# Attention ahead of two MLP stages: global values copied at a step's end, low words shifted on ScalarE, three working buffers for doubles

## The chip, the cores and the metric

One core of a Trainium2 chip runs the whole program. The metric is the device time of one execution in microseconds (us), the median of several runs. The core's engines work side by side, each through a queue of its own in order: PE (TensorE), DVE (VectorE), ACT (ScalarE), POOL (GpSimd) and SP (SyncE, which only issues DMAs here). An instruction that waits holds up all that stand behind it in its engine's queue.

## The reference

```
scores = q @ k.T / 8, for 4 batches x 8 heads x 768 tokens x 64
keep   = (key < 8, the globals) or (0 <= query - key < 96, the local ones)
a      = softmax(where(keep, scores - slope[head] * distance, -1e9))
x      = (a @ v) as 3072 rows of 512
x      = each row through one of 8 experts (512 -> 1024 -> 512, ReLU),
         chosen by sorting all gate values, 384 rows each
out    = two_sided_leaky(x @ w_in) @ w_out     # 512 -> 2048 -> 512
```

The two matrices of the last stage, w_in and w_out, come in as doubles (64 bits); everything else is float32.

## The kernel before

The program first does the attention (about 220 us), then routes the rows, then sends each expert's rows through both MLP stages. Only the attention part is touched.

Attention runs in 48 steps, two for each tile of 128 tokens (`g`), each with four of the eight heads (`u` is 0 or 1). `attention` writes out by hand the order in which each engine gets its work. In step n the queues hold: the scores of step n+1 (L212, tile a_s) on PE; bias and minimum on DVE (L218, a_sx); four exponentials on ACT (L221, a_p); transposes of the probabilities of step n on PE (L232, a_pt), copied out by DVE (L236) and ACT (L234); the product with the gate of step n-2 (L277, a_cb); the transposes of later keys and queries (L169, a_tp); and the values matmul of step n-1 (L248, a_xp). PE is thus a step or two ahead of what the other engines finish.

A key tile sees 104 older keys, of which the first 8 are replaced by the global ones. `place_globals` (L190, tile a_kz) copies the global keys into their places on POOL, two steps ahead of the scores that read them. `place_values` (L196, tile a_v, 32x256) does the same for the global values: it overwrites the first rows of the tile before the step's own, after the values matmul at the end of the step before has read them; the values matmul at the end of the next step reads what was copied. `divisor` (L259) is a small add on POOL.

The doubles are turned into float32 on the side by `Doubles`, as a generator that `attention` advances twice in a step, in four steps of five (PACE). A job is 128x512 doubles, 32 jobs in all, alternately of w_in and w_out. `load` (L67) brings the raw words to a tile f_raw with three slots. At a step's first advance `begin` takes the magnitude of the high word on ACT (L73, into tile f_t), clamps it on POOL (L74) and shifts the low word on POOL (L75, into tile f_r); L73 stands ahead of the exponentials of step n+1. `finish` of the job before, if that was one of w_in, splits it on POOL into two parts (L87, L88). At the second advance, at the step's end, `join` shifts and merges the high word on DVE (L79, L80) and adds the low one on POOL (L82). f_t and f_r have two buffers each, so L73 of a job waits until the job two before has been read for the last time, by L88 or L82.

SP's queue holds in this order what a step issues: the loads of k and q or of v, the store of finished rows, and L67 for a later job.

Of the kernel before, what the change touches and what calls it, by code (L numbers as in the profile page):

```python
# [12 lines left out]
I32 = mybir.dt.int32  # L13
U32 = mybir.dt.uint32
U16 = mybir.dt.uint16
AF = mybir.ActivationFunctionType
OP = mybir.AluOpType
# [13 lines left out]
class Doubles:  # L31
# [36 lines left out]

    def begin(self, job):
        nc, raw = self.nc, job["raw"]  # L70
        t = job["t"] = self.pool.tile([128, self.WIDTH], I32, name="f64_t")
        r = job["r"] = self.pool.tile([128, self.WIDTH], I32, name="f64_r")
        nc.scalar.activation(t.bitcast(FT), raw[:, :, 1].bitcast(FT), AF.Abs, scale=LIFT)  # L73
        nc.gpsimd.tensor_scalar(t.bitcast(FT), t.bitcast(FT), BIG, FLOOR, op0=OP.min, op1=OP.max)  # L74
        nc.gpsimd.tensor_scalar(r, raw[:, :, 0].bitcast(U32), 2.0 ** -29, 1.0, op0=OP.mult, op1=OP.mult)  # L75

    def join(self, job):
        nc, t = self.nc, job["t"]
        nc.vector.tensor_scalar(t, t, 3, 0x7FFFFFF8, op0=OP.logical_shift_left, op1=OP.bitwise_and)  # L79
        nc.vector.scalar_tensor_tensor(t, job["raw"][:, :, 1], -0x80000000, t, op0=OP.bitwise_and, op1=OP.bitwise_or)  # L80
        dst = t if job["dst"] is None else job["dst"].bitcast(I32)
        nc.gpsimd.tensor_tensor(dst, t, job["r"], op=OP.add)  # L82

    def finish(self, job):
        if job["hi"] is not None:
# [5 lines left out]
def attention(ctx, tc, q, k, v, w_gate, n_global, n_local, ident, x_dram, logits, side, router):  # L91
    nc = tc.nc
# [12 lines left out]
    scale = 1.0 / math.sqrt(D)  # L105
# [17 lines left out]
    def load_kq(g):  # L123
        load(g, (("k", k), ("q", q)), 3)

    def load_v(g):
        b, t = divmod(g, NT)
        load(g, (("v", v),), 4)
        if not t:
            nc.sync.dma_start(vg[C - GW:C - W, b % 2], dram_ap(v, b * H * S * D, [[D, G], [S * D, H], [1, D]]))  # L130
# [16 lines left out]
    for r, c0, base, fill in ((rel, G, W, MASKED), (rel0, 0, 0, float(W)), (rel0, G, -G, MASKED)):  # L147
        n = {0: G}.get(c0, r.shape[1] - c0) if r is rel0 else KW - c0
# [23 lines left out]
    def transpose_k(g):  # L172
        t = g % NT
        nc.scalar.activation(kz[:, :, t * C:(t + 1) * C], transpose_in(T["k", g]), AF.Copy)
# [5 lines left out]
    def place_globals(g, u):  # L180
        b, t = divmod(g, NT)
        if t == 0:
            return
        if t == 1 and u == 0:
            kg = work.tile([C, NP, G], FT, name="a_kg", bufs=2)
            nc.gpsimd.tensor_copy(kg, kz[:, :, :G])
            T["KG", b] = kg
        c0 = t * C - GW
        ps = slice(2 * u, 2 * u + 2)
        nc.gpsimd.tensor_copy(kz[:, ps, c0:c0 + G], T["KG", b][:, ps])  # L190

    def place_values(g, u):
        b, t = divmod(g, NT)
        if t:
            hs = slice(4 * u, 4 * u + 4)
            nc.gpsimd.tensor_copy(T["v", g - 1][:C - W, hs], vg[:, b % 2, hs])  # L196

    def scores(g, u):
        b, t = divmod(g, NT)
        if t:  # L200
            c0, n, bs = t * C - GW, KW, bias
        else:
            c0, n, bs = 0, C, bias0
        ps = [psum.tile([C, 2, KW], FT, name=f"a_s{s}") for s in range(2)]
        if u == 0:
            T["sum", g] = work.tile([C, H], FT, name="a_sum", bufs=3)
            T["mn", g] = work.tile([C, H], FT, name="a_mn", bufs=3)
        for a in range(2):
            p = 2 * u + a
            for s in range(2):  # L210
                r = slice(s * D, (s + 1) * D)
                nc.tensor.matmul(ps[s][:, a, :n], T["Q", g][r, p], kz[r, p, c0:c0 + n], start=True, stop=True)  # L212
        for a in range(2):
            sx = work.tile([C, 2, KW], FT, name="a_sx", bufs=2)
            pr = T["P", g, 2 * u + a] = pbuf[:, 2 * u + a]
            for s in range(2):
                h = 2 * (2 * u + a) + s
                nc.vector.tensor_tensor_reduce(out=sx[:, s, :n], in0=ps[s][:, a, :n], in1=bs[:, h], scale=-scale,  # L218
                                               scalar=BIG, op0=OP.add, op1=OP.min,
                                               accum_out=T["mn", g][:, h:h + 1])  # L220
                nc.scalar.activation(pr[:, s, 2 * C - n:], sx[:, s, :n], AF.Exp, bias=T["mn", g][:, h:h + 1],  # L221
                                     scale=-1.0, accum_out=T["sum", g][:, h:h + 1])
# [34 lines left out]
    def divisor(g, u):  # L257
        e = T["se", g, u] = work.tile([C, 4], FT, name="a_se", bufs=4)
        nc.gpsimd.tensor_scalar(e, T["sum", g][:, 4 * u:4 * u + 4], 1e-9, None, op0=OP.add)  # L259

    def norm(g, u):
        r = T["r", g, u] = work.tile([C, 4], FT, name="a_r", bufs=2)
        nc.vector.reciprocal(r, T.pop(("se", g, u)))

    def store(g):
        nc.sync.dma_start(x_dram[g * C:(g + 1) * C, :], T["xo", g])

    def combine(g, u):
        xt = T.pop(("xt", g, u))
        last = g == NG - 1  # L270
        if last and u:
            ps = psum.tile([C, NP, C], FT, name="a_tp", bufs=2).rearrange("c p d -> c (p d)")
            ps = ps[:, :2 * CB].rearrange("c (a d) -> c a d", a=2)
        else:
            ps = psum.tile([C, 2, CB], FT, name="a_cb")
        for a in range(2):
            nc.tensor.matmul(ps[:, a], xt[:, a], cmb[:, 2 * u + a], start=True, stop=True)  # L277
        if not u:
            T["xo", g] = work.tile([C, HD], FT, name="a_xo", bufs=2)
            T["lp", g] = work.tile([C, H, E], FT, name="a_lp", bufs=2)  # L280
        if not last:
            norm(g, u)
        r = T.pop(("r", g, u))
        rr = r.rearrange("c (a s) -> c a s", a=2)
        xo = T["xo", g].rearrange("c (a s d) -> c a s d", s=2, d=D)[:, 2 * u:2 * u + 2]
        nc.vector.tensor_tensor(
            T["lp", g].rearrange("c (a s) e -> c a s e", s=2)[:, 2 * u:2 * u + 2],
            ps[:, :, C:].rearrange("c a (s e) -> c a s e", s=2),
            rr[:, :, :, None].to_broadcast([C, 2, 2, E]), op=OP.mult)
        if last:  # L290
            for i in range(4):
                nc.scalar.activation(xo[:, i // 2, i % 2], ps[:, i // 2, i % 2 * D:(i % 2 + 1) * D], AF.Copy,
                                     scale=r[:, i:i + 1])
        else:
            nc.vector.tensor_tensor(xo, ps[:, :, :C].rearrange("c a (s d) -> c a s d", s=2),
                                    rr[:, :, :, None].to_broadcast([C, 2, 2, D]), op=OP.mult)
        if u:
            nc.vector.tensor_reduce(logits[:, g, :], T["lp", g].rearrange("c h e -> c e h"), axis=AX.X, op=OP.add)
            if g < NG - 2:
                T["store"] = g  # L300
            else:
                store(g)

    def turn(n):
        return 2 <= n < N - 3 and n % PACE[1] < PACE[0]
# [3 lines left out]
    N = len(steps)  # L309
# [10 lines left out]
    for n in range(N + 2):  # L320
        if n < N:
            g, u = steps[n]
            if u == 0 and n and g + 3 < NG:
                load_kq(g + 3)
            if u == 1 and g + 2 < NG:
                load_v(g + 2)
            if "store" in T:
                store(T.pop("store"))
            nx = steps[n + 1] if n + 1 < N else None
            if n + 2 < N:  # L330
                place_globals(*steps[n + 2])
            place_values(g, u)
            if turn(n):
                next(side)
            if nx:
                scores(*nx)
            transpose_p(g, u, 0)
            transpose_p(g, u, 1)
            divisor(g, u)
            if n >= 2:  # L340
                combine(*steps[n - 2])
            if n and g + 2 < NG:
                (transpose_q if u else transpose_k)(g + 2)
        if n == 0:
            transpose_k(2)
            load_kq(3)
        if n == N:
            norm(*steps[n - 2])
            norm(*steps[n - 1])
        if 1 <= n <= N:  # L350
            values(*steps[n - 1])
        if n == N:
            router.start()
        if n >= N:
            combine(*steps[n - 2])
        if turn(n):
            next(side)
        else:
            next(setup, None)
# [821 lines left out]
```

## Time and profile before

| | us |
|---|---|
| median of 3 runs | 1121.75 (1120.18 to 1121.84) |
| the profiled execution's own time | 1119.95 |
| its span, from the first instruction to the last | 1118.2 |
| granted clock of TensorE, mean over the span | 0.976 |
| busy in the span: PE, DVE, ACT, POOL | 1065.7, 762.9, 385.6, 540.5 |

The profile is of one execution. Busy times are those of an engine's own instructions; an engine that is busy for a small share of the whole can still set the pace of a part. A wait is given with the instruction that ended it.

### The profile page before, as it was taken

Reading aid. Unit: us, or ns where it says so; the run is one execution under the profiler, and the core shown is the slowest. Engines: PE = TensorE matmul, PEld = TensorE weight load, DVE = VectorE, ACT = ScalarE, POOL = GpSimd, SP = SyncE. Lnnn points to the kernel's source line nnn. Section 1 sums busy time; section 2 is a strip of 40 time slices with the busy share of each in tenths; the row PEclk is TensorE's granted clock in tenths of the full one; section 3 lists DMA queues with packets and bytes.
Section 4 is the critical chain, followed back from the end, with each engine's and each line's share of the span. In section 5 each row is a group of like instructions: output and inputs, shape, how many; then the busy total and the mean of one; then the engine's idle time right before and its main releaser. Section 6 shows DMA issues by size and latency. Waiting matters only on the chain.

```text
span 1118.2 us, 19406 instructions
## 1 busy us (share of the span) xinstructions
PE 1065.7 (95%) x6659; PEld 944.2 (84%) x6659; DVE 762.9 (68%) x2228; ACT 385.6 (34%) x969; POOL 540.5 (48%) x652
## 2 busy tenths in 40 slices
PE   8989898869999999999999999999999999999997
PEld 6777677648888998899889988898899999999995
DVE  7989888778897878897789698778753323231321
ACT  7777777503322320232133113211331233123211
POOL 4888878315455823462346325432543354236222
PEclk9999999968999999999999999999999999999999
DMA  9788877114135525441534533533353435434131
GB/s 219 212 218 223 209 202 187 49 46 134 57 132 179 173 83 181 130 160 58 198 96 149 163 123 109 157 135 129 95 180 123 133 108 185 131 116 167 57 131 67
DMA packets 151219, 156.55 MB, mean 140 GB/s; under 512 B 83536, under 2 KB 116304, under 8 KB 151120
## 3 DMA queue, kind: packets, MB, share of 16 engines
q1 hardware_dynamic: 147280, 142.72, 42.3%
q0 software_dynamic: 3840, 12.59, 3.4%
q8 instruction: 53, 0.87, 0.3%
q14 instruction: 46, 0.38, 0.1%
HBM read 134.31 MB, written 20.97 MB: 139 GB/s over the span
## 4 chain that ended last, share of the span: by engine, by line
PE 75%; DVE 12%; POOL 6%; issue 3%; ACT 2%; DMA 2%; SPq 0%; DVEq 0%; POOLq 0%; ACTq 0%
PE m_h L963 23%; PE m_acc L988 23%; PE m_h L923 9%; PE m_acc L950 9%; PE a_s L212 2%; PE a_pt L232 2%; PE a_xp L248 2%; DVE r_thr L564 2%; DVE r_red L778 1%; DVE r_cmp L770 1%; PE r_ps L704 1%; POOL wo L82 1%; ACT a_p L221 1%; PE a_cb L277 1%; PE a_tp L169 1%
## 5 line engine op out<-in xcount | busy, mean ns | idle before, releaser
L973 POOL TENSOR_TENSOR m_g<-m_t,m_g 128x384 fp32r<-128x384 f32 (+1 forms) x144 | 140.2, 973 | 372.1 <-ACT m_g L972 369.1
L988 PE MATMUL m_acc<-m_so,m_g 128*128 128x512 f32 x1152 | 298.7, 399 | 0.4 <-POOL m_spacer L996 0.3
L963 PE MATMUL m_h<-m_y,wi 128*128 128x384 f32 x1536 | 294.4, 341 | 0.0
L963 PEld LDWEIGHTS m_h<-m_y,wi 128*128 128x128 f32 x1536 | 273.3, 189 | 7.5
L988 PEld LDWEIGHTS m_acc<-m_so,m_g 128*128 128x128 f32 x1152 | 209.6, 189 | 35.3 <-POOL m_g L973 0.9
L972 ACT ACTIVATE m_g<-m_t 128x384 fp32r<-128x384 f32 (+1 forms) x144 | 70.5, 490 | 435.6 <-DVE m_t L971 255.1
L891 POOL TENSOR_TENSOR m_s<-m_r,m_s 128x512 fp32r<-128x512 f32 x128 | 166.9, 1308 | 103.5 <-ACT m_s L890 103.2
L970 DVE TENSOR_SCALAR m_t<-m_h,m_al 128x384 f32<-128x384 f32 (+1 forms) x144 | 82.2, 571 | 149.2 <-PE m_h L963 136.1
L950 PE MATMUL m_acc<-m_hh,m_s 128*128 128x384 f32 x768 | 150.3, 340 | 1.3 <-DVE m_hh L927 1.3
L923 PE MATMUL m_h<-m_xt,m_s 128*128 128x384 f32 x768 | 146.1, 338 | 0.0
L923 PEld LDWEIGHTS m_h<-m_xt,m_s 128*128 128x128 f32 x768 | 136.4, 190 | 1.9 <-ACT m_xt L872 0.3
L950 PEld LDWEIGHTS m_acc<-m_hh,m_s 128*128 128x128 f32 x768 | 132.4, 188 | 2.9 <-DVE m_hh L927 1.6
L890 ACT ACTIVATE m_s<-m_r 128x512 fp32r<-128x512 f32 x128 | 79.7, 626 | 98.8 <-PE m_acc L950 34.1
L221 ACT ACTIVATE a_p<-a_sx,a_mn 128x232 f32<-128x232 f32 (+1 forms) x192 | 88.5, 462 | 25.8 <-DVE a_mn L218 25.4
L927 DVE SCALAR_TENSOR_TENSOR m_hh<-m_h,m_hh 128x384 fp32r<-128x384 f32 x64 | 35.4, 552 | 76.8 <-ACT m_hh L926 76.2
L971 DVE SCALAR_TENSOR_TENSOR m_t<-m_h,m_t 128x384 f32<-128x384 f32 (+1 forms) x144 | 73.9, 513 | 4.9
L778 DVE TENSOR_REDUCE r_red<-r_cmp 128x24 bf16<-128x576 bf16 (+1 forms) x97 | 73.9, 761 | 3.4
L218 DVE CUSTOM_DVE_ANT_0 a_sx<-a_s,a_bias 128x232 f32<-128x232 f32 (+1 forms) x192 | 61.4, 374 | 11.6 <-PE a_s L212 9.4
L212 PE MATMUL a_s<-a_kz,a_qz 64*128 64x232 f32 (+1 forms) x384 | 50.2, 381 | 18.7 <-POOL a_kz L190 16.2
L926 ACT ACTIVATE m_hh<-m_h 128x384 fp32r<-128x384 f32 x64 | 31.5, 492 | 95.6 <-PE m_h L923 82.3
L770 DVE TENSOR_TENSOR r_cmp<-r_mk,r_thr 128x576 bf16<-128x576 uint16 x78 | 61.4, 787 | 0.0
L212 PEld LDWEIGHTS a_s<-a_kz,a_qz 64*128 64x128 f32 x384 | 33.2, 193 | 28.6 <-POOL a_kz L190 22.6
(183 smaller groups left out, 1283.3 us busy)
## 6 DMA issues: line engine op xcount, KB each, us to landing
m_so<-wo_pairs SPq DMA_DIRECT2D x112, 512.0 KB, 3.3
m_r<-in_moe_w_dram SPq DMA_DIRECT2D x128, 256.0 KB, 3.0
f_raw<-in_moe_w_in_dram SPq DMA_DIRECT2D x16, 512.0 KB, 4.6
f_raw<-in_moe_w_out_dram SPq DMA_DIRECT2D x16, 512.0 KB, 3.7
wo_pairs<-m_so SPq DMA_DIRECT2D x16, 512.0 KB, 2.6
a_k<-in_k_dram SPq DMA_DIRECT2D x24, 256.0 KB, 4.8
a_q<-in_q_dram SPq DMA_DIRECT2D x24, 256.0 KB, 5.2
a_v<-in_v_dram SPq DMA_DIRECT2D x24, 256.0 KB, 4.8
```

Source lines behind the costliest of these rows:

```text
L212: nc.tensor.matmul(ps[s][:, a, :n], T["Q", g][r, p], kz[r, p, c0:c0 + n], start=True, stop=True)
L221: nc.scalar.activation(pr[:, s, 2 * C - n:], sx[:, s, :n], AF.Exp, bias=T["mn", g][:, h:h + 1], scale=-1.0, accum_out=T["sum", g][:, h:h + 1])
L778: nc.vector.tensor_reduce(red, cmp, axis=AX.X, op=OP.add)
L890: self.nc.scalar.activation(s[:, 0], r, AF.Copy)
L891: self.nc.gpsimd.tensor_tensor(s[:, 1], r, s[:, 0], op=OP.subtract)
L923: nc.tensor.matmul(ps[:, :n], s1[:, a, d], x[:, b, d], start=(d == 0 and i == 0), stop=(d == self.ND - 1 and i == 2))
L950: nc.tensor.matmul(ps[:, :n], s2[:, b, d * 128:(d + 1) * 128], h[:, a], start=(f == 0 and a + b == 0), stop=(last and a == 1))
L963: nc.tensor.matmul(ps[:, :n], self.wi[:, a, d, f * 128:(f + 1) * 128], y[:, b, d], start=(d == 0 and i == 0), stop=(d == self.ND - 1 and i ...
L970: nc.vector.tensor_scalar(t[:, cs], ps[:, cs], 0.0, self.al[:, f:f + 1], op0=OP.min, op1=OP.mult)
L971: nc.vector.scalar_tensor_tensor(t[:, cs], ps[:, cs], 0.0, t[:, cs], op0=OP.max, op1=OP.add)
L973: nc.gpsimd.tensor_tensor(g[:, 1, cs], t[:, cs], g[:, 0, cs], op=OP.subtract)
L988: nc.tensor.matmul(ps, g[:, a, t * 128:(t + 1) * 128], s[:, b], start=(f == 0 and a + b == 0), stop=(last and a == 1))
```

## The change

Three edits. The shift of the low word goes from POOL (L75, tile f_r) to ACT, where it writes its result over the raw words; the add of `join` reads it there, and tile f_r is gone. f_t has three buffers instead of two. The copy of the global values is queued at the end of a step, behind the values matmul of the step before, instead of near its beginning. One line less stands in the file above `attention`, so L73 to L331 of before are one lower in the changed kernel, but for the shift itself, which is L74 there.

```
     def begin(self, job):
         nc, raw = self.nc, job["raw"]
-        t = job["t"] = self.pool.tile([128, self.WIDTH], I32, name="f64_t")
-        r = job["r"] = self.pool.tile([128, self.WIDTH], I32, name="f64_r")
+        t = job["t"] = self.pool.tile([128, self.WIDTH], I32, name="f64_t", bufs=3)
         nc.scalar.activation(t.bitcast(FT), raw[:, :, 1].bitcast(FT), AF.Abs, scale=LIFT)
         nc.gpsimd.tensor_scalar(t.bitcast(FT), t.bitcast(FT), BIG, FLOOR, op0=OP.min, op1=OP.max)
-        nc.gpsimd.tensor_scalar(r, raw[:, :, 0].bitcast(U32), 2.0 ** -29, 1.0, op0=OP.mult, op1=OP.mult)
+        nc.scalar.activation(raw[:, :, 0], raw[:, :, 0].bitcast(U32), AF.Copy, scale=2.0 ** -29)
 
     def join(self, job):
...
-        nc.gpsimd.tensor_tensor(dst, t, job["r"], op=OP.add)
+        nc.gpsimd.tensor_tensor(dst, t, job["raw"][:, :, 0], op=OP.add)
...
             if n + 2 < N:
                 place_globals(*steps[n + 2])
-            place_values(g, u)
             if turn(n):
                 next(side)
...
         if n >= N:
             combine(*steps[n - 2])
+        if n < N:
+            place_values(g, u)
         if turn(n):
             next(side)
```

On POOL, one step with doubles in which a job of w_in is finished stood like this before (f_t and f_r are the working tiles of a job, wi and wo the finished matrices, a_se the divisor):

```order
L190 COPY a_kz<-a_kg 128x2x8
L196 COPY a_v<-a_vg 32x256
L74 TENSOR_SCALAR f_t<-f_t 128x512
L75 TENSOR_SCALAR f_r<-f_raw 128x512
L87 TENSOR_SCALAR wi<-f_t 128x512
L88 TENSOR_TENSOR wi<-f_t,wi 128x512
L259 TENSOR_SCALAR a_se<-a_sum 128x4
L82 TENSOR_TENSOR wo<-f_t,f_r 128x512
```

The same place on POOL in the changed kernel:

```order
L189 COPY a_kz<-a_kg 128x2x8
L73 TENSOR_SCALAR f_t<-f_t 128x512
L86 TENSOR_SCALAR wi<-f_t 128x512
L87 TENSOR_TENSOR wi<-f_t,wi 128x512
L258 TENSOR_SCALAR a_se<-a_sum 128x4
L195 COPY a_v<-a_vg 32x256
L81 TENSOR_TENSOR wo<-f_t,f_raw 128x512
```

The shift is gone from POOL's queue, and the copy of the global values stands between the divisor and the last add instead of second.

On ACT, around the exponentials of one step (a_p), before:

```order
L252 ACTIVATE a_xt<-a_xp 128x256
L73 ACTIVATE f_t<-f_raw 128x512
L221 ACTIVATE a_p,a_sum<-a_sx,a_mn 128x232 x4
L234 ACTIVATE a_pts_568<-a_pt_567 128x512
L178 ACTIVATE a_qz<-a_tp 128x512
```

The same place on ACT in the changed kernel:

```order
L251 ACTIVATE a_xt<-a_xp 128x256
L72 ACTIVATE f_t<-f_raw 128x512
L74 ACTIVATE f_raw<-f_raw 128x512
L220 ACTIVATE a_p,a_sum<-a_sx,a_mn 128x232 x4
L233 ACTIVATE a_pts_565<-a_pt_564 128x512
L177 ACTIVATE a_qz<-a_tp 128x512
```

The shift has come in between the magnitude and the four exponentials, 32 times in all. The orders of PE, DVE and SP are as before; on SP the load L67 now waits for POOL alone (and the DMA slot), where it waited for DVE, ACT and POOL, of which DVE's L80 read last.

## Rows read from the trace of the kernel before

**Rows 1.** The page: busy tenths in 40 equal slices of the span.

```profile
PE   8989898869999999999999999999999999999997
POOL 4888878315455823462346325432543354236222
```

**Rows 2.** Timeline of PE, 88 to 111 us: start, length, what, count [idle before].

```profile
93.97 1.05 PE L212 MATMUL a_s<-a_kz,a_qz 64*128 64x232 f32 x8
...
97.94 1.05 PE L212 MATMUL a_s<-a_kz,a_qz 64*128 64x232 f32 x8
```

**Rows 3.** Windows: length, then busy PE, PEld, DVE, ACT, POOL (count); clock, DMA.

```profile
22.17:202.56 180.39, 161.30 (x1531) 132.73 (x1529) 156.40 (x601) 139.07 (x453) 149.97 (x247) 0.96 0.78 203
22.17:44.40 22.23, 20.17 (x202) 16.68 (x201) 20.01 (x74) 18.21 (x59) 18.46 (x37) 1.00 0.91 241
44.40:49.98 5.58, 5.58 (x40) 4.60 (x40) 4.08 (x15) 4.71 (x17) 4.58 (x11) 0.69 0.73 165
93.97:105.92 11.95, 11.95 (x123) 9.99 (x121) 11.57 (x48) 10.43 (x34) 9.20 (x16) 1.00 0.70 190
123.80:133.94 10.14, 8.25 (x80) 6.69 (x80) 9.62 (x34) 7.36 (x26) 9.32 (x16) 1.00 0.86 236
```

**Rows 4.** Waits, 22.17 to 202.56 us: total us, times, longest.

```profile
ACT f_t L73 <- POOL wi L88: 21.0, 12, 3.1
ACT a_p L221 <- DVE a_mn L218: 19.7, 27, 1.3
PE a_s L212 <- POOL a_kz L190: 16.2, 12, 2.7
DVE f_t L79 <- POOL f_t L74: 11.1, 9, 1.9
...
PEld a_pt L232 <- ACT a_p L221: 5.6, 18, 0.7
```

**Rows 5.** Timeline of all engines, 121 to 150 us.

```profile
123.80 0.20 POOL L190 COPY a_kz<-a_kg 128x16 f32<-128x16 f32 x1
...
132.38 0.66 ACT L73 ACTIVATE f_t<-f_raw 128x512 f32<-128x512 f32 x1 [2.50 <-POOL wi L88]
...
133.94 0.20 POOL L190 COPY a_kz<-a_kg 128x16 f32<-128x16 f32 x1
...
134.20 1.05 PE L212 MATMUL a_s<-a_kz,a_qz 64*128 64x232 f32 x8 [1.89 <-POOL a_kz L190]
```

**Rows 6.** Groups by form, 22.17 to 202.56 us: busy us, mean ns, idle before.

```profile
L75 POOL TENSOR_SCALAR f_r<-f_raw 128x512 int32<-128x512 uint32 x32 | 25.1, 784 | 2.5
...
L73 ACT ACTIVATE f_t<-f_raw 128x512 f32<-128x512 f32 x31 | 20.9, 676 | 21.1 <-POOL wi L88 21.0
L82 POOL TENSOR_TENSOR f_t<-f_t,f_r 128x512 int32<-128x512 int32 x16 | 20.5, 1278 | 5.2 <-DVE f_t L80 4.0 <-DVE a_mn L218 0.4
...
L234 ACT ACTIVATE a_pts<-a_pt 128x512 f32<-128x512 f32 x35 | 20.1, 576 | 0.0
L74 POOL TENSOR_SCALAR f_t<-f_t 128x512 f32<-128x512 f32 x32 | 19.7, 615 | 11.3 <-ACT f_t L73 9.3
```

**Rows 7.** Timeline of ACT, 100 to 112 us.

```profile
103.53 0.67 ACT L73 ACTIVATE f_t<-f_raw 128x512 f32<-128x512 f32 x1
...
110.61 0.68 ACT L73 ACTIVATE f_t<-f_raw 128x512 f32<-128x512 f32 x1 [2.34 <-POOL wi L88]
111.20 0.38 ACT L221 ACTIVATE a_p<-a_sx,a_mn 128x128 f32<-128x128 f32 x1
```

**Rows 8.** Single lines, 0 to 222 us: ns min/median/max, first and last start.

```profile
L75 POOL TENSOR_SCALAR f_r<-f_raw x32: 659/680/954, 22.3 to 197.4; 128x512 int32<-128x512 uint32 x32
...
L80 DVE SCALAR_TENSOR_TENSOR f_t<-f_raw,f_t x32: 691/1015/1643, 23.3 to 197.8; 128x512 int32<-128x512 int32 x32
```

**Rows 9.** A load's issue in SP's timeline; page's DMA issues: KB each, us to landing.

```profile
95.37 0.37 SPq L67 DMA_DIRECT2D f_raw<-in_moe_w_out_dram  x1
...
f_raw<-in_moe_w_in_dram SPq DMA_DIRECT2D x16, 512.0 KB, 4.6
```

More of the change, by code (lines that the diff above doesn't have):

```diff
@@ L70, in begin @@
         nc, raw = self.nc, job["raw"]
-        t = job["t"] = self.pool.tile([128, self.WIDTH], I32, name="f64_t")
-        r = job["r"] = self.pool.tile([128, self.WIDTH], I32, name="f64_r")
+        t = job["t"] = self.pool.tile([128, self.WIDTH], I32, name="f64_t", bufs=3)
         nc.scalar.activation(t.bitcast(FT), raw[:, :, 1].bitcast(FT), AF.Abs, scale=LIFT)
         nc.gpsimd.tensor_scalar(t.bitcast(FT), t.bitcast(FT), BIG, FLOOR, op0=OP.min, op1=OP.max)
-        nc.gpsimd.tensor_scalar(r, raw[:, :, 0].bitcast(U32), 2.0 ** -29, 1.0, op0=OP.mult, op1=OP.mult)
+        nc.scalar.activation(raw[:, :, 0], raw[:, :, 0].bitcast(U32), AF.Copy, scale=2.0 ** -29)
     def join(self, job):
@@ L81, in join @@
         dst = t if job["dst"] is None else job["dst"].bitcast(I32)
-        nc.gpsimd.tensor_tensor(dst, t, job["r"], op=OP.add)
+        nc.gpsimd.tensor_tensor(dst, t, job["raw"][:, :, 0], op=OP.add)
     def finish(self, job):
@@ L331, in attention @@
                 place_globals(*steps[n + 2])
-            place_values(g, u)
             if turn(n):
@@ L355, in attention @@
             combine(*steps[n - 2])
+        if n < N:
+            place_values(g, u)
         if turn(n):
```

## Prediction

> **What bounds the kernel now.** I read the page first. Of its 40 slices the attention part has the first eight: PE stands there at 0.8 to 0.9 and POOL climbs to 0.8, while behind it PE alone is full and POOL falls back [rows 1]. Every edit lies in the attention part, so I read only that stretch. One step (half the heads of a tile of 128 tokens) with nothing late takes PE 3.97 us: from the scores at 93.97 to those at 97.94 [rows 2]. From the scores at 22.17 to those at 202.56 lie 40 steps, 180.39 us. PE is busy for 161.30 of them, so 19.1 us are idle, and the granted clock is 0.96, which is worth another 0.04 x 180.39 = 7.2 us [rows 3]. About 26 us are the most that any cure can give here, and 154 us the floor. DVE (156.40) and ACT (139.07) are not far below PE, and that will limit the gain.
>
> The waits say who makes PE idle: the scores wait 16.2 us for the copy of the global keys on POOL (L190), nearly all of the 19.1. Beside it ACT waits 21.0 us at L73 for POOL's L88, twelve times, and DVE 11.1 us at L79 for POOL's L74 [rows 4]. All three wait for one queue. Between two copies of global keys two steps apart, at 123.80 and 133.94, lie 10.14 us [rows 5], in which POOL is busy for 9.32 [rows 3]; the rest is gaps between its 14 instructions. That is 5.07 us a step with doubles, 1.1 more than PE needs. POOL loses this through four such steps and makes it good only in the fifth, which has no doubles. The end of one such run shows the damage: ACT's L73, with the exponentials queued behind it, can start only at 132.38, when L88 is done, after 2.50 us idle; POOL's L190 comes at 133.94, and the scores start at 134.20 after 1.89 us idle [rows 5]. A stall also costs clock: the step behind the one at 44.40 takes 5.58 us, at a granted clock of 0.69 [rows 3].
>
> **The change, part by part.**
>
> *The shift leaves POOL.* 32 instructions of 0.784 us [rows 6], 25.1 us, two in each pair, with a gap of about 0.07 us each: 2 x (0.78 + 0.07) = 1.7 us off the pair, 10.14 to 8.4, or 4.2 us a step. Four steps of that and a fifth with three small copies and adds (I allow 1.2) make 18.0 us, under the 19.9 that PE needs for five. Before it was 4 x 5.07 + 1.2 = 21.5. POOL stops being what five steps wait for, and the waits of rows 4 that name it should nearly go.
>
> *The shift goes to ACT*, directly behind L73 and ahead of a step's four exponentials. The trace of before has no such ACT instruction. L73 lasts 0.68 us and the next starts 0.59 behind it (110.61 and 111.20 [rows 7]), so two overlap by 0.09. Bounds: below, 0.48, a contiguous 512-wide copy (L234, 0.576 [rows 6]) less that overlap; above, L73's 0.676 with none. I take 0.59, since the shift reads the same strided tile as L73. It also writes at that stride, of which no row speaks; 0.95, POOL's slowest time for the same operation [rows 8], goes into a rival. 31 of L73 lie in the stretch: 31 x 0.59 = 18.3 us, and ACT's 139.07 become 157.4.
>
> The Trainium skill (ScalarE: Activation LUTs, section What ACT_TABLE_LOAD costs) gives an instruction with immediate scale 186 ns and 0.833 ns an element, and an overlap of 93 ns: 612 ns, 519 net. The trace agrees on the overlap; L73 at 0.676 is above it. By the page the term would be 16.1 us instead of 18.3.
>
> *The third buffer.* L73 of a job needs the buffer of three jobs ago, not two, so POOL may be a step later before ACT waits for it. I expect the 21.0 us wait to vanish; it reaches PE only through the exponentials, in the same stalls, so it is not added.
>
> *The copy of the global values* (L196) moves on POOL behind the divisor (L259) and ahead of L82; nothing is removed. Its reader, the values matmul, comes at the end of the next step, so about a step is spare. That spare step is its cover; without it PE would lose the copy's length, a fraction of a microsecond a step. L74 no longer stands behind a copy that itself waits for PE, and only L82 queues behind it. I count nothing either way.
>
> *DVE.* L80 takes 0.691 us at best and 1.015 in the median [rows 8]. If the slow ones are those that run beside POOL, L75's going frees the jobs without L87 and L88, half of the 32: 16 x 0.3 = 5 us or nothing, so 151 to 156 remain.
>
> The Trainium skill (SBUF — State Buffer, section Who interferes with whom) says that a VectorE instruction with two SBUF inputs contends with a GpSimd one that reads SBUF. L80 and L75 are such a pair, and the two durations of L80 agree. By that rule DVE ends at 151.
>
> *The raw slots.* L67, the load of a later job, now waits for POOL's last read (L82) instead of DVE's L80, at least L82's 1.28 us later, and the k, q, v loads and the store of rows queue behind it on SP. A load at 95.37 serves the L73 at 103.53, 8.16 us on [rows 7, 9], and lands in 4.6 [rows 9]: 3.5 us are spare. Free, with a rival below.
>
> **The sum.** PE's 154, DVE's 151 to 156, ACT's 157.4 and POOL's 150 - 25 = 125 us have to fit; the longest is ACT. How close does the time come to the busiest engine? In the clean stretch from 93.97 to 105.92 PE fills all of it; in the five steps up to 44.40 it fills 20.17 of 22.23, 91% [rows 3]. With three engines level I take the middle, 0.95: 157.4 / 0.95 = 165.7 us, 14.7 less than 180.39. The ends: 157.4 (23 less) at 1.0, 173 (7 less) at 0.91. The router and the experts start from attention's end and keep their work, so the gain goes through in full. The profiled execution took 1119.95 us (span 1118.2), 1.8 below the median of 1121.75: 1119.95 - 14.7 = 1105.3, and 1107 as a median.
>
> **Rivals.**
>
> 1. *ACT takes POOL's place.* The shift delays the exponentials, and the transposes of probabilities already wait for them 5.6 us in 18 places [rows 4]. If each shift shows in full, 18.3 of the 26 us are lost again: 8 gained, 1114. At 0.95 us each, ACT has 168.5, over 0.95 it is 177.4: 3 gained, 1119. Against: ACT idles 19.7 us ahead of exponentials for DVE [rows 4], more than all shifts last. Chance 0.2.
>
> 2. *POOL isn't unloaded.* L82 now reads its second operand at a stride of two words. If that made it half as slow again, 1.28 to 1.92 us, a pair would take 8.4 + 1.3 = 9.7 us, and of the 2.2 us by which a pair exceeds PE's pace 0.4 would be cured: some 4 us, 1118. Against: L75 reads those words in 0.659 us at best [rows 8], L74 contiguous ones in 0.615 [rows 6]. Chance 0.05.
>
> The Trainium skill (GPSIMD Engine Reference, section 7, Performance pitfalls for Q7 kernels) puts half as much again on reads with a step over 8 bytes. Two words are just 8, so by it this rival fails; no row shows the edge.
>
> 3. *Slower: raw slots come free late.* If L82 ends 4.2 us behind L80, where I expect 1.3 to 2.2, a load misses its L73 by 0.64 us. 31 such misses, on ACT and ahead of the exponentials, cost 20 us: 14.7 - 20 = 5 lost, 1127. From 3.5 us of delay it begins, from about 4.0 it decides. For: SP already runs in order behind several waits. Against: POOL should be less late than now. Chance 0.06.
>
> 4. *Nearly all comes back*, 157.4 us: 1098. For: three clean steps in a row exist. Against: they used slack that had built up. Chance 0.12.
>
> **How the numbers follow.** The forecast, 10 to 20 us gained, has the remaining 0.57: 1107, its own range 1102 to 1112. The range reaches rivals 1 and 4 and leaves out rival 3 and the outer end of 4: 1096 to 1119. Within 0.2% (2.2 us, about what a measurement here can tell) lie parts of rivals 1 and 2: 0.07; slower 0.06; faster 0.87.
>
> **What would show it.** Right: the scores' wait for the key copy falls from 16.2 to under 4 us; ACT's wait for L88 is gone; a pair on POOL takes 8.3 to 8.7 us; the shift shows 0.55 to 0.7 us; the attention's granted clock is 0.99. Wrong: the probabilities' transposes wait over 10 us for ACT (1), L82 lasts over 1.5 us (2), L73 waits for the raw load (3). It falls altogether if PE stays as idle while POOL is idle too.

## The result and the profile after

| | before | after |
|---|---|---|
| median, us | 1121.34 (1120.18 to 1121.84, 4 runs) | 1105.05 (1104.53 to 1105.69, 4 runs) |
| profiled execution's own time, us | 1119.95 | 1105.07 |
| span, us | 1118.2 | 1103.4 |
| mean granted clock | 0.976 | 0.982 |

The ratio is 0.9852, with a 95% interval of [0.9837, 0.9866]: 1.5% faster, 16 us. The forecast was 1107.

The page's slices of the changed kernel (busy tenths) answer to [rows 1]:

```profile
PE   8999999689999999999999999999999999999997
POOL 4777776036457623542354326333533364246222
```

PE has nines where it had eights, and POOL stays at seven. The same 40 steps now lie between the scores at 22.93 and those at 187.34. Windows of the changed kernel, columns as in [rows 3]; the second is one step, from one scores to the next:

```profile
22.93:187.34 164.41, 155.22 (x1531) 127.20 (x1529) 154.24 (x597) 152.24 (x479) 126.10 (x212) 1.00 0.85 220
...
120.19:125.07 4.88, 4.25 (x43) 3.31 (x41) 4.84 (x15) 4.31 (x14) 4.51 (x7) 1.00 1.01 248
```

The stretch fell from 180.39 to 164.41 us, 15.98 less; the whole execution fell by 14.88, so 1.1 us of it were lost again, 0.8 of them ahead of the stretch, whose first scores start at 22.93 instead of 22.17. PE is idle for 9.2 us instead of 19.1, and its busy time fell by 6.1 us, with a granted clock of 1.00 instead of 0.96. POOL lost 23.9 us. DVE lost 2.2 and ACT gained 13.2. The waits of the changed kernel over that stretch (total us, times, longest) answer to [rows 4]:

```profile
ACT a_p L220 <- DVE a_mn L217: 12.0, 16, 2.4
PEld a_s L211 <- POOL a_kz L189: 11.8, 14, 2.1
POOL f_t L73 <- ACT f_t L72: 11.6, 8, 2.0
PE a_s L211 <- POOL a_kz L189: 8.6, 12, 1.9
...
PEld a_pt L231 <- ACT a_p L220: 5.2, 18, 0.3
```

ACT's wait for POOL's last product, 21.0 us before, is no longer there; the clamp on POOL waits for ACT, as it did before (11.6 us, and 9.3 in [rows 6]). What is left of the old picture is the wait of the scores for the key copy: 8.6 us, still twelve times. The groups by shape over the same stretch show the instructions that changed:

```profile
L79 DVE SCALAR_TENSOR_TENSOR f_t<-f_raw,f_t 128x512 int32<-128x512 int32 x32 | 25.8, 805 | 1.1
L74 ACT ACTIVATE f_raw<-f_raw 128x512 int32<-128x512 uint32 x31 | 21.7, 701 | 0.0
L78 DVE TENSOR_SCALAR f_t<-f_t 128x512 int32<-128x512 int32 x32 | 21.7, 678 | 1.4 <-POOL f_t L73 1.4
L81 POOL TENSOR_TENSOR f_t<-f_t,f_raw 128x512 int32<-128x512 int32 x16 | 20.8, 1301 | 14.4 <-ACT a_qz L177 5.7 <-ACT a_xt L251 3.5 <-issue 1.9
```

The shift on ACT lasts 0.701 us, and ACT is not idle ahead of it. The add with its strided operand lasts 1.30 us, against 1.28 before [rows 6], so the stride costs it next to nothing.

Where the 8.6 us come from is seen in one step, 120.19 to 125.07. Its timeline, POOL with the instructions of the other engines that it meets (start, length):

```profile
115.78 0.20 POOL L189 COPY a_kz<-a_kg 128x16 f32<-128x16 f32 x1
...
118.27 1.31 POOL L81 TENSOR_TENSOR f_t<-f_t,f_raw 128x512 int32<-128x512 int32 x1 [0.69 <-ACT a_xt L251]
...
119.52 0.20 POOL L189 COPY a_kz<-a_kg 128x16 f32<-128x16 f32 x1
...
119.68 0.61 POOL L73 TENSOR_SCALAR f_t<-f_t 128x512 f32<-128x512 f32 x1
...
120.37 0.62 POOL L86 TENSOR_SCALAR wi<-f_t 128x512 fp32r<-128x512 f32 x1
...
121.07 1.28 POOL L87 TENSOR_TENSOR wi<-f_t,wi 128x512 fp32r<-128x512 f32 x1
...
121.14 1.49 DVE L78 TENSOR_SCALAR f_t<-f_t 128x512 int32<-128x512 int32 x1
...
122.67 0.69 DVE L79 SCALAR_TENSOR_TENSOR f_t<-f_raw,f_t 128x512 int32<-128x512 int32 x1
122.78 0.84 POOL L195 COPY a_v<-a_vg 32x256 f32<-32x256 f32 x1
...
123.59 1.29 POOL L81 TENSOR_TENSOR wo<-f_t,f_raw 128x512 int32<-128x512 int32 x1
...
124.83 0.19 POOL L189 COPY a_kz<-a_kg 128x16 f32<-128x16 f32 x1
...
125.07 0.47 PE L211 MATMUL a_s<-a_kz,a_qz 64*128 64x232 f32 x2 [0.53 <-POOL a_kz L189]
```

A step in which a job of w_in is finished can still have more on POOL than PE's 3.97 us allow: from key copy to key copy 5.31 us here, without a gap of note. The step before it (115.78 to 119.52) takes POOL 3.74, 0.69 of them idle. The mean is now near PE's pace, but the work is uneven, and the key copy stands behind all of it. DVE is as full: 4.84 of 4.88 us, since its L78 needs 1.49 us beside L87 here and 0.43 alone.

### The profile page after: what moved, and what is told of

The parts are those of the page before. It is cut to its first block, busy times and chain, and to the rows that moved or that the text cites. A ratio compares the mean times of both kernels' runs of the same rounds, so it can differ in the third digit from the quotient of the medians.

```text
span 1103.4 us, 19396 instructions
## 1 busy us (share of the span) xinstructions
PE 1059.9 (96%) x6658; PEld 939.1 (85%) x6659; DVE 761.8 (69%) x2228; ACT 401.4 (36%) x1001; POOL 516.1 (47%) x620
## 3 DMA queue, kind: packets, MB, share of 16 engines
q1 hardware_dynamic: 147280, 142.72, 42.9%
## 4 chain that ended last, share of the span: by engine, by line
PE 72%; DVE 14%; ACT 3%; issue 2%; DMA 1%; POOL 1%; SPq 0%; DVEq 0%; ACTq 0%; POOLq 0%
PE m_h L963 24%; PE m_acc L988 24%; PE m_acc L950 9%; PE m_h L923 9%; DVE a_sx L217 2%; DVE r_thr L564 2%; ACT a_p L220 2%; DVE r_red L778 1%; DVE r_cmp L770 1%; PE r_ps L704 1%; PE a_pt L231 1%; PE a_xp L247 1%; PE m_h L857 1%; PE a_s L211 1%; DVE f_t L78 1%
## 5 line engine op out<-in xcount | busy, mean ns | idle before, releaser
L231 PE MATMUL a_pt<-ident,a_p 128*128 128x128 f32 x352 | 50.1, 282 | 0.2
```

## The experiments

The theory at the start, A in the expectations: POOL's queue was the cause, so its 25.1 us are the gain, what is left of the key copy's wait is still POOL's, and the other two edits give little. Against it stood that the gain comes from decoupling, by the buffer (B) or by the order on POOL (C). Later came three more: that the wait which is left is only where another engine's delay shows (D), that ACT, with the shift, now holds the steps (E), and that before the change only the key copy stood in the wrong place (K). Ten runs went to these; two more tried a version that beats both kernels. Ratios are to the kernel before, with 95% intervals.

**Each edit alone.** First the shift alone, with two buffers and the copy in its old place:

```
-        r = job["r"] = self.pool.tile([128, self.WIDTH], I32, name="f64_r")
...
-        nc.gpsimd.tensor_scalar(r, raw[:, :, 0].bitcast(U32), 2.0 ** -29, 1.0, ...)
+        nc.scalar.activation(raw[:, :, 0], raw[:, :, 0].bitcast(U32), AF.Copy, scale=2.0 ** -29)
...
-        nc.gpsimd.tensor_tensor(dst, t, job["r"], op=OP.add)
+        nc.gpsimd.tensor_tensor(dst, t, job["raw"][:, :, 0], op=OP.add)
```

> Of the three edits only the shift of the low words on ScalarE, in place; two buffers and the copy of the global values stay as before. Theory A (POOL's queue was what the attention steps waited for, and what counts is the 25.1 us taken from it): nearly the whole gain, 1104 to 1109 us, the scores' wait for the key copy well under 16.2 us. Theory B (the gain comes from the third buffer, which ends ACT's 21.0 us wait for L88 ahead of the exponentials): little, 1117 to 1122 us. Theory C (it comes from the place of the global values' copy in POOL's queue): little, 1117 to 1122 us.

Measured: 1104.84 us, 0.9866 [0.9849, 0.9882]. Nearly the whole gain is here. ACT's wait for L87 is still there, 7.2 us from 20 to 205 us, and costs nothing that can be measured.

The third buffer alone; f_r goes to one buffer:

```
-        t = job["t"] = self.pool.tile([128, self.WIDTH], I32, name="f64_t")
-        r = job["r"] = self.pool.tile([128, self.WIDTH], I32, name="f64_r")
+        t = job["t"] = self.pool.tile([128, self.WIDTH], I32, name="f64_t", bufs=3)
+        r = job["r"] = self.pool.tile([128, self.WIDTH], I32, name="f64_r", bufs=1)
```

> Of the three edits only the third buffer of f_t. For room f_r gets one buffer instead of two, which costs nothing in theory, since POOL alone writes and reads it, in order. Theory A: POOL still has 10.1 us in a pair of steps, so 1117 to 1122 us, though ACT's wait for L88 goes. Theory B: 1106 to 1111 us. Theory C: 1119 to 1122 us.

Measured: 1121.36 us, 1.0011 [1.0001, 1.0021]. Its waits from 20 to 205 us:

```profile
ACT a_p L221 <- DVE a_mn L218: 42.9, 34, 3.4
...
PE a_s L212 <- POOL a_kz L190: 15.8, 11, 2.7
```

ACT's 21.0 us in front of L73 are gone and stand in front of the exponentials, which now wait 42.9 us instead of 21.7 between the same times. PE's wait is 15.8 instead of 16.2. The wait moved along ACT's queue, and the time stayed.

The later copy of the global values alone, and then together with the third buffer (the changed kernel with the shift still on POOL):

```
-            place_values(g, u)
             if turn(n):
...
+        if n < N:
+            place_values(g, u)
         if turn(n):
```

> Of the three edits only the copy of the global values queued at the end of a step. Theory A: POOL's work is the same, 1117 to 1122 us. Theory B: 1119 to 1122 us. Theory C: 1106 to 1111 us.

> The changed kernel with the shift back on POOL (into f_r with one buffer): third buffer and later copy of the global values, no shift on ScalarE. Theory A: 1114 to 1121 us, since POOL keeps its 25.1 us. Theories B and C, each or together: 1104 to 1109 us, the whole gain without the shift's move.

Measured: 1118.33 us, 0.9984 [0.9975, 0.9994], and 1118.08 us, 0.998 [0.9971, 0.999]. The copy gives 0.2% while POOL is late. The waits of the first of them from 20 to 205 us show why not more:

```profile
PE a_s L212 <- POOL a_kz L190: 10.3, 12, 2.7
...
PE a_xp L248 <- POOL a_v L196: 7.7, 8, 1.3
```

The scores wait 6 us less for the key copy, and the values copy, now late itself, makes PE wait for 7.7 us. Decoupling as the cause falls: without the shift, two edits of three give 0.2%.

**What is left of the key copy's wait.** The copy of a later step is queued at a step's end, ahead of the doubles' add, once in the changed kernel and once in the kernel before:

```
-            if n + 2 < N:
-                place_globals(*steps[n + 2])
+            if not n:
+                place_globals(*steps[2])
...
+        if n + 3 < N:
+            place_globals(*steps[n + 3])
```

> The changed kernel with the copy of the global keys queued on POOL one place earlier: at the end of the step before, ahead of the copy of the global values and of that step's last add, instead of behind that add. Theory A (what is left of PE's idle time, 8.6 us for the key copy, comes from the add of 1.29 us that stands ahead of it and itself waits for DVE): the wait falls under 3 us and the time to 1097 to 1102 us. Rival D (DVE and ACT at 0.93 to 0.94 of the stretch set the pace, and the key copy is only where it shows): the wait moves to the probabilities' transposes or the scores' banks, 1103 to 1106 us.

> The kernel before with the same move of the key copy, and no other edit. Theory A (POOL's sum of work per five steps is too long, 21.5 us against 19.9): the wait of the scores falls, but POOL stays late and PE meets it elsewhere (ACT's L73 behind L88, the values matmul), 1113 to 1120 us. Rival K (POOL's work would fit; only the key copy stands in the wrong place): 1103 to 1109 us, as much as the change gave.

Measured: in the changed kernel 1104.09 us, 0.9857 [0.9841, 0.9874], no gain; in the kernel before 1116.38 us, 0.9964 [0.995, 0.9979]. Window of the changed kernel with this edit:

```profile
23.05:186.37 163.32, 158.72 (x1531) 128.37 (x1529) 153.92 (x596) 151.59 (x476) 128.00 (x211) 1.00 0.85 221
```

Two of its waits:

```profile
PE a_s L211 <- DVE a_mn L217: 2.1, 3, 1.3
...
PE a_s L211 <- POOL a_kz L189: 0.5, 1, 0.5
```

The scores' wait for the key copy falls from 8.6 to 0.5 us, and the 40 steps take 1.1 us less, not 8. A's wait came as expected, its time was missed. In part the scores now wait for DVE to read their banks (2.1 us). For the rest PE is "busy" for 158.72 us instead of 155.22: its groups of matmuls are stretched over the gap, their parts starting a little late (scores of 1.13 us and transposes of 1.23 at 124.19 and 125.26, against 1.05 and 1.09 elsewhere in the same timeline). The long step seen above, 4.88 us from 120.19 to 125.07, and the one behind it show it best. The first window is that next step in the changed kernel, the others are the same two steps in this run:

```profile
125.07:129.14 4.07, 4.07 (x40) 3.35 (x40) 3.84 (x16) 3.57 (x14) 3.07 (x7) 1.00 0.85 228
...
119.77:124.19 4.42, 4.18 (x42) 3.31 (x40) 4.28 (x16) 3.83 (x12) 4.13 (x7) 1.00 0.96 231
124.19:128.73 4.54, 4.45 (x42) 3.42 (x40) 4.40 (x18) 3.91 (x16) 3.50 (x9) 1.00 0.90 242
```

Together the two take 8.95 us there and 8.96 here: the delay only moved into the next step. This is what D says: the wait was where a delay showed, not what made it. While POOL was the bound, the same edit did give 4 us, not the whole gain that K expected.

**Is it ACT?** The shift is left out of the changed kernel (a tile of zeros is added instead), and then made twice, the second into a spare tile:

```
-        nc.scalar.activation(raw[:, :, 0], raw[:, :, 0].bitcast(U32), AF.Copy, scale=2.0 ** -29)
...
-        nc.gpsimd.tensor_tensor(dst, t, job["raw"][:, :, 0], op=OP.add)
+        nc.gpsimd.tensor_tensor(dst, t, self.zero, op=OP.add)
```

```
+        spare = self.pool.tile([128, self.WIDTH], I32, name="f64_spare", bufs=1)
+        nc.scalar.activation(spare, raw[:, :, 0].bitcast(U32), AF.Copy, scale=2.0 ** -29)
```

> The changed kernel without the shift: the low words are left out, and the last add takes a tile of zeros instead, so the weights lose their three lowest bits. ACT loses 32 instructions of 0.70 us. Theory A (the shift lies in time in which ACT waits for DVE): 1102 to 1105 us. Rival E (ACT took POOL's place in part, and each shift shows): 1090 to 1099 us.

> The changed kernel with a second shift of the same shape on ScalarE ahead of the first, into a spare tile that nobody reads: 32 instructions of about 0.70 us more on ACT. ACT then has 152 + 31 x 0.43 to 0.70 = 165 to 174 us of work for a stretch that takes 164. Theory A (one shift fits, and a second is over ACT's slack): 1110 to 1120 us. If ACT still has room: 1105 to 1108 us. Rival E (each shift shows in full, 32 x 0.6): 1122 us or more.

Measured: without it 1103.14 us, 0.9853 [0.9836, 0.9869]; twice 1113.35 us, 0.9945 [0.9928, 0.9962]. Their windows, each of its own 40 steps, first without, then twice:

```profile
23.32:186.86 163.54, 155.11 (x1530) 127.05 (x1529) 153.68 (x597) 135.02 (x444) 124.90 (x212) 1.00 0.85 220
```

```profile
23.25:197.50 174.25, 165.82 (x1530) 128.00 (x1528) 152.07 (x600) 173.11 (x514) 127.52 (x216) 1.00 0.79 207
```

The first shift costs ACT 152.24 - 135.02 = 17.2 us of work and the program nothing that can be measured: the exponentials wait 28.5 us for DVE in the run without it, 12.0 with it. A second shift finds that slack used up: ACT is busy for 99% of the stretch, the 40 steps take 9.8 us more.

Both causes were then taken away together, the shift and the key copy's place (the two edits above):

> The changed kernel with both the earlier key copy and no shift (low words left out, zeros added). Either alone left the time where it was. If the two cover each other (the wait for the key copy and ACT's share each fill the slack the other frees): 1096 to 1100 us. If DVE, at 154 of 164 us, is what both stand behind: 1102 to 1105 us.

Measured: 1102.87 us, 0.9848 [0.9824, 0.9872]. They did not cover for each other: the 40 steps take 162.90 us. Something else holds them there.

**Is it DVE?** The changed kernel without DVE's second instruction of a join, the merge of the sign:

```
-        nc.vector.scalar_tensor_tensor(t, job["raw"][:, :, 1], -0x80000000, t, ...)
```

> The changed kernel without DVE's second instruction of join, L79 (the sign is not merged, so all weights of the last stage come out positive). DVE loses 32 instructions of 0.805 us, 25.8 us, and POOL's add can start that much earlier. If DVE's end of the step is what the key copy and the exponentials stand behind: 1092 to 1099 us, the scores' wait for the key copy under 3 us. If ACT with the shift sets the pace: 1102 to 1105 us.

Measured: 1093.59 us, 0.976 [0.9739, 0.9782]. Its window and two of its waits (line numbers one lower from L79 on):

```profile
23.24:177.31 154.07, 152.47 (x1530) 127.03 (x1528) 127.89 (x568) 151.91 (x480) 121.41 (x214) 1.00 0.89 234
```

```profile
DVE a_sx L216 <- PE a_s L210: 15.3, 24, 1.3
...
PEld a_s L210 <- POOL a_kz L188: 2.4, 4, 1.2
```

The 40 steps are at PE's floor, 154 us. DVE waits for PE now, and the key copy's wait has gone too, though nothing was done to the copy. ACT's work is the same as in the changed kernel, so ACT at 152 us does not keep PE from its floor. But this run takes away two things, 26 us of DVE and the place where that instruction holds up POOL's copies. A meeting of DVE's other instruction with POOL's last product of w_in is still in it, and its step shows what that alone does:

```profile
115.64 1.25 DVE L78 TENSOR_SCALAR f_t<-f_t 128x512 int32<-128x512 int32 x1
...
115.18:119.14 3.96, 3.96 (x43) 3.33 (x41) 3.74 (x14) 3.96 (x13) 3.65 (x7) 1.00 0.93 255
```

L78 is stretched to 1.25 us, DVE still fits with 3.74, and the step lasts 3.96.

**A version that beats both kernels?** If DVE's time is what counts, 5 us of it moved to POOL should help. The logits' sum over the heads goes there as three small adds, in the changed kernel and in the one with the earlier key copy:

```
-            nc.vector.tensor_reduce(logits[:, g, :], T["lp", g]..., axis=AX.X, op=OP.add)
+            lp = T["lp", g]
+            nc.gpsimd.tensor_tensor(lp[:, :4], lp[:, :4], lp[:, 4:], op=OP.add)
+            nc.gpsimd.tensor_tensor(lp[:, :2], lp[:, :2], lp[:, 2:4], op=OP.add)
+            nc.gpsimd.tensor_tensor(logits[:, g, :], lp[:, 0], lp[:, 1], op=OP.add)
```

> The changed kernel with the logits' sum over eight heads (L297, one reduction on DVE in every second step, 5.2 us over the 40 steps) made by three adds on POOL, queued behind the copy of the global values and ahead of the last add; DVE 154.2 becomes 149, POOL 126 becomes some 139 (60 adds of about 0.2 us). If DVE's end of the step sets the pace after the change (as the run without L79 says: 26.3 us less DVE gave 11.5 us), 2 to 5 us come off: 1100 to 1103, and the 40 steps take 160 to 163. Rival: POOL's queue counts again, since its adds wait for DVE and the add of the doubles stands behind them: same time or up to 3 us longer, 1105 to 1108, with the key copies' wait above 8.6.

> The same, and the key copy is queued ahead of the doubles' add, so that no matmul waits for that add. If DVE sets the pace: 1099 to 1102, a little under the run with the later adds alone, since POOL's longer queue can't reach the scores. Rival (POOL): here too no gain over 1104.

Measured: 1111.02 us, 0.9916 [0.9902, 0.9929], and 1107.95 us, 0.9892 [0.9877, 0.9907]. Both are slower than the changed kernel. Two windows of the first, the 40 steps and one step with w_in's end and the adds:

```profile
23.31:194.30 170.99, 157.93 (x1531) 129.90 (x1529) 150.87 (x577) 152.73 (x478) 144.51 (x272) 0.98 0.81 211
...
124.32:129.97 5.65, 4.25 (x42) 3.31 (x41) 5.33 (x17) 5.37 (x18) 5.12 (x10) 1.00 0.93 233
```

Part of that step, from its timeline:

```profile
123.65 0.20 POOL L189 COPY a_kz<-a_kg 128x16 f32<-128x16 f32 x1
...
125.21 1.44 POOL L87 TENSOR_TENSOR wi<-f_t,wi 128x512 fp32r<-128x512 f32 x1
...
125.54 1.66 DVE L79 SCALAR_TENSOR_TENSOR f_t<-f_raw,f_t 128x512 int32<-128x512 int32 x1
...
127.36 0.25 POOL L298 TENSOR_TENSOR a_lp<-a_lp 128x32 f32<-128x32 f32 x1
...
128.14 0.39 POOL L195 COPY a_v<-a_vg 32x256 f32<-32x256 f32 x1
...
128.57 0.88 PE L247 MATMUL a_xp<-a_pts,a_v 128*64 128x128 f32 x12 [0.88 <-POOL a_v L195]
...
129.73 0.19 POOL L189 COPY a_kz<-a_kg 128x16 f32<-128x16 f32 x1
129.97 1.05 PE L211 MATMUL a_s<-a_kz,a_qz 64*128 64x232 f32 x8 [0.52 <-POOL a_kz L189]
```

DVE's busy time fell by 3.4 us and the steps got longer by 6.6: the rival, POOL's queue, held, and by more than it had said. The adds fall into the step that is already the longest on POOL (key copy to key copy 6.08 us here, 5.31 without them; the adds hold POOL's queue for 0.78, from 127.36 to 128.14), and PE waits in it for the values and again for the keys. With the earlier key copy the scores wait for it only 0.8 us, and the values matmul still waits 5.4 us for its copy.

## Why the prediction was right

**The cause.** It said that one queue, POOL's, is what the waits stand for, and that taking the shift off it is worth the lag. The shift alone gave 0.9866, the other two edits 0.998.

**The size.** 40 steps in 165.7 us were forecast, 164.41 measured, and the median is 1105.05 against 1107. The working was: the longest engine over 0.95. The longest is DVE with 154.24 and not ACT, and 154.24 / 164.41 is 0.94. The step that names ACT as the engine that sets the time was wrong: without the shift ACT has 135.02 us, and the steps take 163.54. So the mechanism, POOL's queue, was right, and that the time came within 1.3 us of the forecast is in part luck. ACT's term was 5.2 us too large: "31 x 0.59 = 18.3 us, and ACT's 139.07 become 157.4" came as 17.2 us for the shifts themselves, 0.555 each, on an ACT that without them needs 135.02 in the faster stretch, not 139.07. And DVE's "5 us or nothing" came as nothing: the merge (L80 before, L79 after) fell from 0.951 to 0.805 us in the mean, 4.6 us in all, and the shift ahead of it (L79 before, L78 after) rose from 0.532 to 0.678, together 47.4 us before and 47.5 after. The merge no longer meets POOL's shift; the shift on DVE now takes over 0.9 us nine times, each time beside POOL's last product of w_in (L87), where it did so once before. The two groups of the kernel before, from the same view as [rows 6]:

```profile
L80 DVE SCALAR_TENSOR_TENSOR f_t<-f_raw,f_t 128x512 int32<-128x512 int32 x32 | 30.4, 951 | 1.1
...
L79 DVE TENSOR_SCALAR f_t<-f_t 128x512 int32<-128x512 int32 x32 | 17.0, 532 | 11.2 <-POOL f_t L74 11.1
```

The share of 0.95, the middle of two bounds, was what carried the forecast, and it was an estimate. The granted clock, forecast at 0.99, came as 1.00.

**The pair on POOL.** 8.3 to 8.7 us were forecast. The pair from 115.78 to 124.83 takes 9.05, more than that; 0.69 of it is one wait, and 8.36 are work and gaps. What the mean hid is that the two steps of a pair are not equal, 3.74 and 5.31 us.

**The key copy.** "Falls from 16.2 to under 4 us" was wrong: 8.6 are left, for the reason just given. It did not spoil the time, since removing the wait gives nothing that can be measured.

**Third buffer and later copy.** Counted at nothing beside the shift. The buffer takes ACT's wait of 21.0 us away, as forecast, but alone it only moves it along ACT's queue; the later copy is worth 0.2% while POOL is late. The spare step that was to cover it did not hold there (PE waits 7.7 us for the values), and holds in the changed kernel (0.3 us, of a weight load alone). In the changed kernel the two together are worth nothing that the runs can tell (1105.05 with them, 1104.84 without).

**The rivals.** ACT in POOL's place (1) fell with the runs without the shift, and the run with a second shift shows how near it was: one more cost 9.8 us over the 40 steps. The strided add (2) fell: 1.30 us. Late raw slots (3): no wait of ACT for a raw load is listed. Nearly all back (4) is where the run without the sign's merge went, and past it, to 154.07 us for the 40 steps.

**What stays open.** After the change DVE (154 us), ACT (152) and PE (155) are level, and in the step that ends a job of w_in DVE and POOL are both full. The trace of the changed kernel says where the time above PE's floor lies. Six of the 40 steps last over 4.5 us (from 59.34, 80.23, 120.19, 141.03, 161.42 and 182.68 on); the longest of them, and the sum of the six:

```profile
161.42:166.63 5.21, 3.60 (x32) 2.89 (x33) 5.07 (x17) 3.60 (x12) 4.12 (x6) 1.00 0.91 226
...
sum 28.97, PE 23.43 PEld 18.70 DVE 28.21 ACT 25.11 POOL 26.15; mean PE 3.90 PEld 3.12 DVE 4.70 ACT 4.18 POOL 4.36
```

They are 5.2 us longer than six of PE's 3.97, half of the 10.4 us by which the stretch is over 154. DVE is busy for 97% of them, and in each one of its two instructions of a join is stretched beside L87, to 0.98 to 1.64 us. This speaks for a meeting that costs a step only where it leaves DVE no room, but it is read from traces and not shown by a run: the one run that freed the steps took away DVE's work and most of the meetings, and moving DVE's work to POOL made POOL late. So no version that beats both kernels was found: the earlier key copy in the changed kernel (0.9857) can't be told from it.

## What to carry to other kernels

Read which queue the waits name, and take work off that queue first: the decoupling edits here (a buffer, an order) only moved the wait, along ACT's queue or from the keys to the values, as long as POOL's work was too long. After such a move, look at the longest single step of each engine and not at its mean; three small adds there, 0.78 us of POOL's queue, made the step 0.77 us longer, from 4.88 to 5.65. And a wait that is left after the bound has moved may only be the place where another engine's delay shows: take it away alone before counting on it.

## What the runs showed of the hardware

DVE and POOL stretch each other, and it shows as busy time and not as waits. DVE's L78, one input and 0.43 us alone, took 1.49 beside POOL's L87 and ended 0.28 us behind it; DVE's L79, with two inputs, takes 0.69 alone and 1.66 beside L87 (in the run with the adds); POOL's copy of the values takes 0.39 alone and 0.84 when L79 started first. Taking POOL's shift away did not lower the sum over the two DVE instructions, it only changed which of them meets POOL. The Trainium skill (SBUF — State Buffer, Who interferes with whom) says that the one that issues first has the shared ports for its whole instruction and that the other blocks; these three pairs agree nearly, also in that a one-input tensor_scalar can be concerned: each blocked instruction ends 0.13 to 0.15 us sooner than its own length behind the end of the other. By its rule for two inputs the prediction's sentence expected DVE to end at 151. The merge did fall by the 4.6 us, but L78 rose by 4.7, and the measured 154.24 decides: the rule tells that the two contend, not that less work on one of them means fewer meetings.

A shift on ACT that reads and writes 512 words at a stride of two lasts 0.70 us, and 31 of them add 17.2 us to ACT's busy time, 0.555 each. A second one, from such words into a contiguous tile, lasts 0.69 us and adds 20.9 us, 0.67 each, in a stretch where ACT is busy for 99%.
